# A windowed-attention and feed-forward kernel: two chunks' feed-forward in halves of d_ff, scores two pairs ahead, byte decoding of weights

## The chip, the cores and the metric

The kernel runs on one core of a Trainium2 chip: TensorE (matmuls, into PSUM), VectorE (DVE), ScalarE (ACT), GpSimd (POOL), and SyncE (SP), whose queue issues most of the transfers. The metric is the device time in microseconds of one execution, median of the runs.

## What is computed

Attention with 4 sink positions and a window of 128 over 768 positions, 4 batches, 8 heads of 64 dimensions, then a feed-forward net of d_model 512 and d_ff 2048 on all 3072 tokens. The weights of the net are given as f64.

```python
keep = is_sink | in_window           # pos < 4, or 0 <= i - j < 128
scores = np.where(keep, scale * q @ k.T, -1e9)
a = softmax(scores)
x = (a @ v).transpose(0, 2, 1, 3).reshape(B * S, H * D)
h = x @ w_in
g = np.where(h >= 1, h, np.where(h <= -1, 0.0, (h + 1) ** 2 / 4))
out = g @ w_out
```

## The kernel before

The tokens are cut into 8 chunks of 384 (`CT` = 3 tiles of 128 positions): first half of the sequence for each of the 4 batches, then the second half. A chunk needs 8 *units*, one per head. The result of a chunk's attention lands in `xn` (L245) as four column blocks `ct`, one for each pair of heads.

**Attention of the first 16 units** (chunks 0 and 1) is done in 8 *pairs* of heads, in plain f32: `pair_load` (L408) brings q and k by two transfers, `pair_values` (L418) the values by four, `pair_scores` (L431) multiplies, masks and takes the row's peak on VectorE (L452) and the exponential on ScalarE (L457); `pair_sums` (L460) makes the reciprocals of the row sums; `early_transp` (L468) transposes the probabilities on TensorE, with ScalarE copies out of PSUM (L477, L478, L480); `pair_r` (L498) spreads the reciprocals over 64 partitions by 12 matmuls (L505), `pair_av` (L482) multiplies with the values and VectorE scales the result (L496). The later units take `load`, `scores`, `values`, `transp`, `av`, `sinks` (L254 to L405), in which operands are split into a high and a low part for faster matmuls.

**The feed-forward net** of a chunk is `moe_steps` (L621): four `split`s of `xn` into high and low parts `x` (L618 on ScalarE, L619 on VectorE); then for each of 16 slices `j` of d_ff `stage1` (12 matmuls, L588, 3 for each `ct`; then L595 to L598 and the low part `gl`, L599, which is on POOL for chunk 0 and on VectorE later), and `LAG` = 2 slices behind it `stage2` (9 matmuls, L607, into three PSUM banks `o_ps`, evicted and stored after the last slice, L614, L615). The last two slices' `stage2` are the `tail`, worked in at the start of the next chunk.

**Weights** are f64 in memory. A step `weights(n)` (L194) decodes two slices of `w_in` (n even) or `w_out` (n odd): a transfer of 1 MB (`fetch`, up to two steps ahead, on SP's queue for the first four, on ScalarE's after that), then `decode_parts` (L164): a shift (L170), the sign bits (L176) and the low word's bits (L179) on VectorE, a rounding copy `high` on ScalarE (L180), and the rest on VectorE (L183).

**Order.** TensorE runs in the order in which the program is written. VectorE and ScalarE are ordered by a planner, except where `queue` (L64) chains an instruction behind the one before on its engine. `first_pairs` (L523) writes out pairs 0 to 3, pair 4's scores and four weight steps (`WFIRST`) by hand. After it, `spread` (L637) mixes step lists in proportion to their weights: the feed-forward net of chunk 0 with the other 12 weight steps, and that with pairs 5 to 8 (`pair_steps`, L509) and units 16 and 17. From then on each chunk's feed-forward net is mixed with the attention of the next chunk. `recheck` (L230) loads the weights again and compares their exponents, once per unit from unit 24 (`CHECK`).

## Time and profile before

| | |
|---|---|
| median of 3 runs | 706.29 us (705.91 to 710.62) |
| the profiled execution | 705.98 us |
| its span, first to last instruction | 704.3 us |
| mean granted clock of TensorE | 0.994 |
| TensorE busy | 681.5 us |
| VectorE busy | 510.3 us |
| ScalarE busy | 489.5 us |
| POOL busy | 278.8 us |

The profile is one execution. PE is TensorE's matmuls, PEld its weight loads, which overlap with the matmuls. A group of instructions has its line, its engine, what it writes and reads, and a count; the idle time ahead of it is put down to whatever released it last. The ends of matmuls are modelled, so a matmul that waits behind another also counts as busy. Times within the execution are us from the span's start.

### The profile page before, as it was taken

What the parts mean: (1) busy time and instruction counts of PE and PEld (TensorE: products, weight loads), DVE (VectorE), ACT (ScalarE), POOL (GpSimd) and SP (SyncE); (2) the same over time, 40 slices, a digit from 0 to 9 for tenths busy, and PEclk for the clock granted to TensorE, in tenths of its full rate; (3) what the DMA queues carried; (4) which work ended last, traced back from release to release, by engine and by line L of the source; (5) the groups of instructions that cost most, each with busy time, mean ns of one, the idle gap of its engine ahead of it and who ended that gap; (6) DMA issues with size and microseconds to landing.
All of it is one profiled execution on the core that took longest, in us unless ns stands there. A gap on an engine that the chain in (4) does not pass through costs nothing.

```text
span 704.3 us, 12263 instructions
## 1 busy us (share of the span) xinstructions
PE 681.5 (97%) x3889; PEld 604.6 (86%) x3889; DVE 510.3 (72%) x1405; ACT 489.5 (70%) x1241; POOL 278.8 (40%) x470
## 2 busy tenths in 40 slices
PE   5899998999999999999999999999999999999996
PEld 3567877899999999989889999899899999989995
DVE  7888998887776877688777878878787877642221
ACT  4886667687778868777787877777776876554332
POOL 3003344744443445355554455635544444300000
PEclk9899999999999999999999999999999999999999
DMA  7864533132244344254333443434322310001001
GB/s 232 291 216 156 190 99 135 49 107 60 63 148 124 102 127 129 68 174 128 92 113 105 147 130 124 126 118 133 122 59 62 102 50 22 3 1 45 1 1 49
DMA packets 45441, 73.98 MB, mean 105 GB/s; under 512 B 10744, under 2 KB 30008, under 8 KB 45368
## 3 DMA queue, kind: packets, MB, share of 16 engines
q1 hardware_dynamic: 42104, 60.53, 28.2%
q10 hardware_dynamic: 3264, 12.58, 4.8%
q8 instruction: 33, 0.54, 0.3%
q14 instruction: 40, 0.33, 0.1%
HBM read 66.80 MB, written 6.29 MB: 104 GB/s over the span
## 4 chain that ended last, share of the span: by engine, by line
PE 79%; DVE 9%; DMA 3%; ACT 3%; POOL 3%; issue 2%; SPq 0%; ACTq 0%; POOLq 0%; DVEq 0%
PE h_ps L588 33%; PE o_ps L607 32%; PE ps_a L283 4%; PE ps_a L390 4%; PE ps_a L344 2%; DVE bits L176 2%; DVE bits L179 1%; DMA w<-w_in 1%; POOL q_l L269 1%; PE ps_a L474 1%; DVE w L183 1%; DVE bits L170 1%; PE ps_a L493 1%; DVE p L304 1%; DVE g L597 1%
## 5 line engine op out<-in xcount | busy, mean ns | idle before, releaser
L588 PE MATMUL h_ps<-x,wi 128*128 128x384 f32 x1536 | 310.2, 340 | 0.0
L588 PEld LDWEIGHTS h_ps<-x,wi 128*128 128x128 f32 x1536 | 262.2, 188 | 8.7 <-issue 1.5
L607 PE MATMUL o_ps<-w,gh 128*128 128x512 f32 x768 | 244.0, 398 | 0.0
L607 PE MATMUL o_ps<-w,gl 128*128 128x512 f32 x384 | 151.1, 393 | 0.4 <-POOL gl L599 0.4
L607 PEld LDWEIGHTS o_ps<-w,gh 128*128 128x128 f32 x768 | 134.3, 188 | 16.9 <-issue 1.7
L597 DVE SCALAR_TENSOR_TENSOR g<-g,h_ps 128x384 f32<-128x384 f32 x128 | 70.3, 549 | 61.7 <-ACT g L596 60.6
L595 ACT ACTIVATE g<-h_ps,half 128x384 f32<-128x384 f32 x128 | 73.9, 578 | 52.7 <-PE h_ps L588 52.0
L269 POOL TENSOR_TENSOR q_l<-r,q_h 128x384 fp32r<-128x384 f32 x48 | 51.1, 1064 | 122.7 <-ACT q_h L268 116.1
L598 ACT CAST gh<-g 128x384 fp32r<-128x384 f32 x128 | 65.5, 512 | 46.1 <-DVE g L597 44.9
L290 ACT ACTIVATE p<-p,peak 128x260 f32<-128x260 f32 (+1 forms) x144 | 71.5, 496 | 23.0 <-DVE peak L287 22.4
L607 PEld LDWEIGHTS o_ps<-w,gl 128*128 128x128 f32 x384 | 72.0, 188 | 17.8 <-POOL gl L599 0.7
L599 DVE TENSOR_TENSOR gl<-g,gh 128x384 fp32r<-128x384 f32 x112 | 67.3, 601 | 23.5 <-ACT gh L598 22.6
L267 DVE TENSOR_TENSOR k_s<-k_r,k_s 64x524 fp32r<-64x524 f32 (+1 forms) x44 | 49.1, 1115 | 34.4 <-ACT k_s L265 34.3
L596 ACT ACTIVATE g<-g 128x384 f32<-128x384 f32 x128 | 67.0, 524 | 2.0
L287 DVE CUSTOM_DVE_ANT_0 p<-ps_a,m 128x260 f32<-128x260 f32 (+1 forms) x144 | 57.0, 407 | 14.7 <-PE ps_a L283 13.8
L358 POOL TENSOR_SCALAR_AFFINE_SELECT pt<-pt 128x384 fp32r<-128x384 f32 (+1 forms) x96 | 51.3, 535 | 22.6 <-DVE pt L349 19.5
L304 DVE CUSTOM_DVE_ANT_0 p<-p,stat 128x128 f32<-128x128 f32 x128 | 57.0, 489 | 0.2
L356 POOL TENSOR_SCALAR_AFFINE_SELECT pt<-pt 128x384 fp32r<-128x384 f32 (+1 forms) x96 | 49.9, 521 | 8.8 <-ACT pt L348 4.9
L599 POOL TENSOR_TENSOR gl<-g,gh 128x384 fp32r<-128x384 f32 x16 | 23.4, 1461 | 67.7 <-ACT gh L598 64.2
L390 PEld LDWEIGHTS ps_a<-pt,v_s 128*128 128x128 f32 x304 | 42.4, 190 | 1.8
L390 PE MATMUL ps_a<-pt,v_s 128*128 128x256 f32 (+1 forms) x304 | 41.9, 275 | 0.0
L283 PE MATMUL ps_a<-k_s,q_h 128*128 128x260 f32 (+1 forms) x144 | 40.7, 283 | 1.2 <-DVE sk L352 0.9
(151 smaller groups left out, 933.1 us busy)
## 6 DMA issues: line engine op xcount, KB each, us to landing
r<-qk SPq DMA_DIRECT2D x48, 192.0 KB
k_r<-qk SPq DMA_DIRECT2D x32, 262.0 KB
again<-w_in SPq DMA_DIRECT2D x16, 512.0 KB
again<-w_out SPq DMA_DIRECT2D x16, 512.0 KB
w<-w_in ACTq DMA_DIRECT2D x6, 1024.0 KB
w<-w_out ACTq DMA_DIRECT2D x6, 1024.0 KB
out<-o SPq DMA_DIRECT2D x23, 256.0 KB
r<-vx SPq DMA_DIRECT2D x32, 128.0 KB
```

The source lines that it names most:

```text
L269: nc.gpsimd.tensor_tensor(q_l, q_r, q_h.bitcast(F32), op=ALU.subtract)
L283: nc.tensor.matmul(ps[:, lo:260], lhsT=q[:, i * P:(i + 1) * P], rhs=k_s[:, c0:c0 + 260 - lo], start=(j == 0), stop=(j == len(qs) - 1))
L290: nc.scalar.activation(p[:, i, lo:260], p[:, i, lo:260], AF.Exp, bias=peak_i, scale=-1.0, accum_out=stat[:, i:i + 1])
L304: nc.vector.tensor_tensor_reduce(out=own, in0=own, in1=p[:, i, 0:P], scale=r, scalar=0.0, op0=ALU.add, op1=ALU.add, accum_out=stat[:, i:i ...
L390: nc.tensor.matmul(z, lhsT=w, rhs=y, start=(n == 0), stop=(n == len(mms) - 1))
L588: nc.tensor.matmul(h_ps[:, :T], lhsT=w_i[j][:, w, ct * P:(ct + 1) * P], rhs=x[:, y, ct], start=(ct == 0 and n == 0), stop=(ct == NCT - 1 a ...
L595: nc.scalar.activation(g, h_ps[:, :T], AF.Relu, bias=half, scale=0.5)
L596: nc.scalar.activation(g, g, AF.Square)
L597: nc.vector.scalar_tensor_tensor(g, g, 1.0, h_ps[:, :T], op0=ALU.min, op1=ALU.max)
L598: nc.scalar.copy(gh, g)
L599: (nc.gpsimd if row0 == GL_POOL else nc.vector).tensor_tensor(gl, g, gh.bitcast(F32), op=ALU.subtract)
L607: nc.tensor.matmul(o_ps[tt], lhsT=gg[:, tt * P:(tt + 1) * P], rhs=w_o[j][:, w], start=(j == 0 and n == 0), stop=(j == NJ - 1 and n == 2))
```

## The change

- *Halves of d_ff.* The feed-forward nets of chunks 0 and 1 are done in two halves, slices 0 to 7 and 8 to 15, in the order 0 front, 1 front, 0 back, 1 back. The front's sums go from PSUM to memory (`half_o`, six blocks of 128x512), and are read back and added by VectorE at the end of the back half. Chunk 1 has an `xn1` of its own, so that both can be split again for the back halves.
- *Weights.* Three decodings instead of four in the head, seven in chunk 0's front, four in chunk 1's front, two in chunk 0's back. The transfer of the first steps is no longer ahead of its step.
- *Byte decoding.* The shift and sign steps are replaced by two one-operand byte operations, which write bytes 0 and 3 of each word of `ends`; one two-operand step then makes the word, in place of the low word in the loaded tile.
- *Head.* Scores of pairs 0 and 1 come first, then those of pair m + 2 in step m; decoding and splits are put elsewhere, and the first stage of slices 0 and 1 for blocks `ct` 0 to 2 comes ahead of pair 3's values. The splits of `ct` 0 and 1 copy on POOL; the copies L478 of the first eight heads are on VectorE.
- *Loads.* q and k of a pair or unit in one transfer, a pair's values in one; the sink values need no transfer of their own. Later units' loads are kept behind the pairs' loads. q and v have separate raw tiles.
- *Scaled pairs.* Pairs 5 to 7 scale the probabilities on VectorE ahead of the transposes, need no `pair_r`, and their result is copied by ScalarE.
- `gl` is always on VectorE; the 1e-9 addition of units 16 and 17 is on VectorE; `recheck` begins at unit 26.

```diff
@@ constants
-GL_POOL = 0
-CHECK = range(24, 24 + 2 * NJ)
-WFIRST = 4
+SCALED = range(5, NATIVE // 2)
+CHECK = range(26, 26 + 2 * NJ)
+WFIRST = 3
+WSPLIT = (10, 14)
+HALF = NJ // 2
...
+    def decode_parts(t, ends, words, w, on, early):
...
+        b = words.bitcast(U8).rearrange("p j c (w e) -> p j c w e", e=4)
+        e = ends.rearrange("p j c -> p (j c)").bitcast(U8).rearrange("p (j c e) -> p j c e", j=2, e=4)
...
+            first = nc.vector.tensor_scalar(e[..., 0], b[..., 0, 3], 5, 0x07, op0=ALU.logical_shift_right,
+                                            op1=ALU.bitwise_and)
...
+            second = nc.vector.tensor_scalar(e[..., 3], b[..., 1, 3], 0x80, 0xC0, op0=ALU.bitwise_and,
+                                             op1=ALU.bitwise_xor)
...
+            queue(nc.vector.scalar_tensor_tensor(w, x, 3, ends, op0=ALU.logical_shift_left, op1=ALU.bitwise_xor), early)
...
-            return decode_parts(t, dec.tile([P, 2, DM], I32, name=f"bits{n % 2}"), words, pin=not on, on=on)
+            return decode_parts(t, ends, words, ends if n == NP - 1 else words[..., 0], on, n < WFIRST + 2)
...
-        loaded.append(nc.sync.dma_start(k_s, qkp[b, h // 2, :, T:T + W]).ins)
-        nc.sync.dma_start(q_s, qkp[b, h // 2, :, 0:T])
+        loaded.append(queue(nc.sync.dma_start(qk_s, qkp[b, h // 2, :, :T + W])).ins)
...
+        if m in SCALED:
+            for a in range(2):
+                for i in range(CT):
+                    p = early_p(2 * m + a)[:, i, KB if i == 0 else 0:260]
+                    nc.vector.tensor_scalar(p, p, r[:, a, i:i + 1], None, op0=ALU.mult)
...
+            if u < H:
+                queue(nc.vector.tensor_copy(spn[u % 2][:NSINK], ps[:NSINK, 2 * P:CT * P]))
...
+        for m in (0, 1):
+            for i in range(CT):
+                pair_scores(m, i)
...
+        for m in range(n):
+            pair_load(m + 2)
+            if m < n - 1:
+                wsteps[m + 1][0]()
+            pair_values(m + 1)
+            pair_sums(m)
+            if m == n - 1:
+                head[2][1]()
+                d[m - 1][4]()
+            if 0 < m < WFIRST:
+                block(m)
+            for u in (2 * m, 2 * m + 1):
+                for part in range(2):
+                    early_transp(u, part)
+            if m < n - 1:
+                hold = later if m + 2 == n else None
+                pair_scores(m + 2, 0, hold)
+                pair_scores(m + 2, 1, hold)
+                last = []
+                pair_scores(m + 2, 2, last)
+                pair_r(m)
...
+                if not m:
+                    block(m)
+                else:
+                    d[m - 1][4]()
+                mult = pair_av(m)
+                mult()
+                d[m][3]()
+                if m:
+                    head[m - 1][1]()
+            else:
+                for _, f in head[CT:]:
+                    f()
...
+                pair_r(m)
+                pair_av(m)()
...
-        (nc.gpsimd if row0 == GL_POOL else nc.vector).tensor_tensor(gl, g, gh.bitcast(F32), op=ALU.subtract)
+        nc.vector.tensor_tensor(gl, g, gh.bitcast(F32), op=ALU.subtract)
...
+    def sums_of(row0, tt):
+        o = parts[row0, tt] = moe.tile([P, DM], F32, name="o")
+        nc.sync.dma_start(o, half_o[row0, tt])
...
+            if put == 2:
+                o = parts.pop((row0, tt))
+                nc.vector.tensor_tensor(o, o_ps[tt], o, op=ALU.add)
...
+            if put == 1:
+                half_o[row0, tt] = dram.tile([P, DM], F32, name=f"half{row0}_{tt}")
+                nc.sync.dma_start(half_o[row0, tt], o)
...
+            if put == 2 and tt == 0:
+                sums_of(row0, 2)
...
+        if on and ct < 2:
+            nc.gpsimd.tensor_copy(x[:, 0, ct], xs[:, ct])
...
+    front, back = range(HALF), range(HALF, NJ)
...
+    prev = moe_steps(rows[0], tail, True, xn, front, 1)
+    cut = CT + LAG * (NCT - 1)
+    finish = first_pairs(prev[:cut])
+    pairs = [pair_steps(m) for m in range(5, 9)]
...
+    prev = spread(decoding(WFIRST, WSPLIT[0]), prev[cut + 2 + LAG:], WLEAD)
+    for _, f in spread(pairs, prev, LEAD):
+        f()
+    prev = spread(decoding(*WSPLIT), moe_steps(rows[1], tail, False, xn1, front, 1), WLEAD)
+    for _, f in spread([step for n in (NATIVE, NATIVE + 1) for step in attn_steps(n)], prev, LEAD):
+        f()
+    n0 = NATIVE + 2
+    prev = spread(decoding(WSPLIT[1], NP), moe_steps(rows[0], tail, False, xn, back, 2), WLEAD)
+    prev += moe_steps(rows[1], tail, False, xn1, back, 2)
```

## Rows read from the trace of the kernel before

**Rows 1.** The page, part 1: busy us, share of the span and instructions of each engine.

```profile
PE 681.5 (97%) x3889; PEld 604.6 (86%) x3889; DVE 510.3 (72%) x1405; ACT 489.5 (70%) x1241; POOL 278.8 (40%) x470
```

**Rows 2.** Windows: length; busy (instructions) of PE, PEld, DVE, ACT, POOL; clock, DMA, GB/s.

```profile
0.00:13.00 13.00, 7.62 (x34) 5.37 (x36) 7.80 (x42) 6.13 (x19) 5.59 (x34) 1.00 0.82 255
13.00:44.00 31.00, 23.89 (x199) 16.39 (x196) 28.59 (x79) 24.79 (x81) 0.91 (x2) 0.89 0.78 261
20.00:24.00 4.00, 4.00 (x24) 2.66 (x24) 3.39 (x9) 2.80 (x10) 0.46 (x1) 0.58 0.63 193
44.00:126.00 82.00, 79.84 (x487) 64.24 (x488) 73.02 (x128) 55.05 (x138) 31.70 (x24) 1.00 0.43 148
120.00:130.00 10.00, 8.06 (x42) 6.80 (x41) 8.49 (x25) 6.06 (x17) 7.74 (x10) 1.00 0.43 134
200.00:300.00 100.00, 99.94 (x563) 91.34 (x562) 74.50 (x221) 77.88 (x200) 44.16 (x84) 1.00 0.36 110
```

**Rows 3.** The chain of waits: start us, us, what.

```profile
111.33 1.45 PE ps_a L493 x16
359.68 3.23 DMA r<-vx
689.48 2.08 PE h_ps L588 x12
691.56 6.17 PE o_ps L607 x27
```

**Rows 4.** Groups of VectorE, 0 to 44 us: busy us, mean ns | idle before.

```profile
L176 DVE SCALAR_TENSOR_TENSOR bits<-w,bits 128x1024 int32<-128x1024 int32 x4 | 4.9, 1216 | 0.0
L170 DVE TENSOR_SCALAR bits<-w 128x1024 int32<-128x1024 int32 x4 | 2.6, 662 | 2.9 <-DMA w<-w_in 2.9
L183 DVE TENSOR_TENSOR wi<-bits,wi 128x1024 fp32r<-128x1024 f32 x2 | 2.5, 1226 | 0.8 <-ACT wi L180 0.8
```

**Rows 5.** Timeline of the head: start us, us, engine, line, operation.

```profile
8.50 0.08 DVE L452 DVE_READ_ACCUMULATOR2_ANT peak<- 128x1 f32 x1
14.76 0.28 DVE L452 CUSTOM_DVE_ANT_0 pt<-o_ps,m 128x128 f32<-128x128 f32 x1
15.88 0.08 DVE L452 DVE_READ_ACCUMULATOR2_ANT peak<- 128x1 f32 x1
43.85 1.83 PE L588 MATMUL h_ps<-x,wi 128*128 128x384 f32 x9
```

**Rows 6.** Groups of TensorE, 44 to 130 us; the last one to 140.

```profile
L505 PE MATMUL ps_a<-ident,stat 128*64 128x128 f32 x48 | 3.5, 281 | 0.0
L344 PE MATMUL ps_a<-ident,p 128*128 128x128 f32 x3 | 0.9, 328 | 1.9 <-DVE p L302 1.9
L607 PE MATMUL o_ps<-w,gl 128*128 128x512 f32 x46 | 18.2, 396 | 0.4 <-POOL gl L599 0.4
```

**Rows 7.** Single lines: count, shortest/median/longest ns, first and last start.

```profile
L239 ACT COPY top<-again x32: 637/658/672, 196.7 to 508.7; 128x512 uint8<-128x512 uint8 x32
L614 ACT COPY o<-o_ps x23: 562/587/594, 142.0 to 697.1; 128x512 f32<-128x512 f32 x23
L126 DVE TENSOR_SCALAR m1n<-m1n x1: 285/285/285, 6.3 to 6.3; 128x260 f32<-128x260 f32 x1
L358 POOL TENSOR_SCALAR_AFFINE_SELECT pt<-pt x96: 402/523/1327, 129.8 to 611.4; 128x384 fp32r<-128x384 f32 x64, 128x256 fp32r<-128x256 f32 x32
```

**Rows 8.** Groups of VectorE from 44, of POOL from 0, to 126 us.

```profile
L176 DVE SCALAR_TENSOR_TENSOR bits<-w,bits 128x1024 int32<-128x1024 int32 x12 | 17.0, 1414 | 0.2
L599 POOL TENSOR_TENSOR gl<-g,gh 128x384 fp32r<-128x384 f32 x13 | 19.6, 1506 | 64.5 <-ACT gh L598 61.1 <-PE ps_a L474 3.5
```

**Rows 9.** Timeline of VectorE and POOL at 80 us.

```profile
80.15 1.00 POOL L599 TENSOR_TENSOR gl<-g,gh 128x384 fp32r<-128x384 f32 x1 [4.52 <-ACT gh L598]
80.16 2.07 DVE L176 SCALAR_TENSOR_TENSOR bits<-w,bits 128x1024 int32<-128x1024 int32 x1
81.46 1.67 POOL L267 TENSOR_TENSOR k_s<-k_r,k_s 64x392 fp32r<-64x392 f32 x1 [0.30 <-ACT k_s L265]
```

More of the change, by code (lines that the diff above doesn't have):

```diff
@@ L185, in decode_parts, with word @@
-        return shift, sign, tail, rest_of
-    def decode(t, w, words, pin=False):
-        for f in decode_parts(t, w, words, pin):
-            f()
+            second = nc.vector.tensor_scalar(e[..., 3], b[..., 1, 3], 0x80, 0xC0, op0=ALU.bitwise_and,
+                                             op1=ALU.bitwise_xor)
+            if not on:
+                tc.keep_in_program_order(second)
+            queue(second, early)
+        def word():
+            queue(nc.vector.scalar_tensor_tensor(w, x, 3, ends, op0=ALU.logical_shift_left, op1=ALU.bitwise_xor), early)
@@ L191, in attn_ffn, with high_of @@
+        def high_of():
+            queue(nc.scalar.copy(high, w.bitcast(F32)), early)
+        def rest_of():
+            queue(nc.vector.tensor_tensor(rest, w.bitcast(F32), high.bitcast(F32), op=ALU.subtract), early)
+        return tail, sign, word, high_of, rest_of
     top = {}
@@ L199, in fetch @@
         def fetch():
-            for k in range(n, min(n + min(AHEAD if n > 2 else 1, NP // 2 - n // 2 - 1) + 1, NP)):
+            for k in range(n, min(n + min(AHEAD if n > 2 else 0, max(NP // 2 - 1 - (n + 1) // 2, 0)) + 1, NP)):
                 if k not in raw:
                     raw[k] = wpool.tile([P, 2, 2 * DM], I32, name="w")
-                    with tc.issue_after(loaded[-1]) if k < SYNC else nullcontext():
-                        (nc.sync if k < SYNC else nc.scalar).dma_start(raw[k], src(k))
+                    queue((nc.sync if k < SYNC else nc.scalar).dma_start(raw[k], src(k)), k < SYNC)
         def parts(on):
@@ L623, in moe_steps, with split @@
+    def split(x, xs, ct, on=False):
+        if on and ct < 2:
+            nc.gpsimd.tensor_copy(x[:, 0, ct], xs[:, ct])
+        else:
+            queue(nc.scalar.copy(x[:, 0, ct], xs[:, ct]), on)
+        queue(nc.vector.tensor_tensor(x[:, 1, ct], xs[:, ct], x[:, 0, ct].bitcast(F32), op=ALU.subtract), on)
+    def moe_steps(row0, tail, first=False, xs=xn, js=range(NJ), put=0):
         x = xpool.tile([P, 2, NCT, CT * P], F32R, name="x")
         o_ps, hs = [], {}
-        steps = [(0.0, lambda ct=ct: split(x, ct)) for ct in range(NCT)]
+        steps = [(0.0, lambda ct=ct: split(x, xs, ct, first)) for ct in range(NCT)]
@@ new lines, in moe_steps @@
+        for n, j in enumerate(js):
+            if n < LAG:
+                steps += second[n * CT:(n + 1) * CT]
+            if n >= LAG or not first:
+                steps += [(0.49, lambda j=j, ct=ct: stage1(x, j, ct, hs)) for ct in range(NCT)]
+            if n >= LAG:
+                steps += [(0.65, lambda j=js[n - LAG], tt=tt: stage2(o_ps, hs, j, tt, row0, js, put)) for tt in range(CT)]
+        if put == 2:
+            steps.append((0.0, lambda: (sums_of(row0, 0), sums_of(row0, 1))))
@@ L634, in moe_steps @@
+        tail[:] = [(0.65, lambda j=j, tt=tt: stage2(o_ps, hs, j, tt, row0, js, put)) for j in js[-LAG:]
                    for tt in range(CT)]
@@ new lines, in decoding @@
+    def decoding(a, b):
+        return [(1.0, wsteps[n][2]) for n in range(a, b)]
+    prev = moe_steps(rows[0], tail, True, xn, front, 1)
+    cut = CT + LAG * (NCT - 1)
+    finish = first_pairs(prev[:cut])
+    pairs = [pair_steps(m) for m in range(5, 9)]
+    for m in (2, 3):
+        pairs[m].append((0.0, lambda u=units[NATIVE + m - 2]: load(u)))
+    pairs = [step for steps in pairs for step in steps]
+    hold = []
+    for _, f in prev[cut + 1:cut + 2]:
+        f()
+    pair_load(6)
+    pair_values(5)
```

283 lines of the change are left out of this document (147 added, 136 removed).

## The prediction

> **What bounds the kernel now.** I read the busy totals first. TensorE is busy for 97% of the span, no other engine for more than 72% [rows 1], so at first sight only fewer matmuls would help. But that share is an average, and a busy matmul can be a slow one, so next come the windows [rows 2]. From 200 to 300 us TensorE is busy 99.94 of 100 us with 563 matmuls, and its weight loads take 91 us. From 0 to 44 us it issues 233, and the loads take 22 us (the first two rows together). So there are two regimes: a steady one from about 44 us, in which TensorE is the limit, and a head, in which something else is.
>
> The chain of waits gives the steady pace: 12 first-stage matmuls take 2.08 us, 27 second-stage ones 6.17, the 16 of one pair's values 1.45 [rows 3]. A slice (12 and 9 of them) is then 4.14 us, and the feed-forward net alone 8 chunks x 16 slices x 4.14 = 530 us, which nothing here makes smaller. What can be won lies where TensorE waits.
>
> In the head VectorE is busy 28.59 of the 31 us from 13 to 44 [rows 2], 92%: there it is the limit. Each of its four weight decodings costs 0.66 + 1.22 + 1.22 + 1.23 = 4.3 us (the two two-operand steps alike), and the first had it wait 2.9 us for a weight transfer [rows 4]. Feed-forward work runs from 43.85 us [rows 5]. From 44 to 126 us VectorE is still busy 73 of 82 us, but TensorE 79.8 [rows 2]. Its one long wait up to 130 us is 1.9 us at unit 16's first transposes, for VectorE's scaling L302, with 0.4 us more for a `gl` on POOL behind it [rows 6]; the window 120 to 130 shows that hole, 8.06 of 10 us busy.
>
> **The change, part by part.** All sums are made against the profiled execution, 705.98 us (span 704.3), 0.3 us under the median of 706.29.
>
> *Head, VectorE's queue.* One decoding of four leaves the head: -4.3 us. In the other three a byte operation of 1024 elements takes the place of the shift (0.66) and a second one that of the sign step (1.22). No row shows a byte operation on VectorE. The nearest are the shift itself, one tensor operand read in steps of 8 bytes, at 0.66 us, and the two-operand form at 1.22 [rows 4]. ScalarE's byte copy in the same steps takes 658 ns for 512 elements, against 587 for 512 f32 out of PSUM [rows 7], so bytes as such are not slow. I take 0.66 for each, as they have one tensor operand, and keep 1.22 as the other end: -0.56 per decoding, -1.7 for three. Eight 4x128 copies move from ScalarE to VectorE: between 0.08 (an accumulator read) and 0.28 (128 wide out of PSUM) [rows 5] I take 0.25, +2.0. So 28.6 - 4.3 - 1.7 + 2.0 = 24.6 us of work. Scores of pairs 0 and 1 now both come ahead of any weight, so this work starts where pair 0's reductions end, 8.5 us [rows 5], not at 12.88. At the same 92% it takes 26.7 us, to 35.2. About 2.5 us idle are within that share: pair 0's transposes need ScalarE copies queued behind the exponentials of two pairs.
>
> The last pair does not end with VectorE. From about 34 us TensorE runs 18 first-stage matmuls put ahead of it (18 x 0.173 = 3.1), pair 3's 12 spreading matmuls (0.7), its 16 of values (1.45); then come the multiplication (0.55) and the last split (1.0): 34 + 0.4 + 3.1 + 0.7 + 1.45 + 0.55 + 1.0 = 41.2, with hops 41.5 us. TensorE is then ahead of where it stands at 43.85 today by 15 first-stage matmuls (2.6 us; three run early today too) and some transposes and scores (0.7). Gain: 43.85 - 41.5 + 3.3 = **5.6 us**. Best end 8 (no hops). [...]
>
> *Transfers.* q and k of a pair become one DMA, its values one in place of four. On SP's queue each weight transfer from w1 on stands behind a pair's q and k, which wait for the scores two pairs back. By my order w0 is wanted at 15.4 us and is the fourth transfer, 2.0 MB in all: 8 us at the 255 GB/s of the first 13 us [rows 2]. w1 makes it 3.6 MB, about 15 us, wanted at 19. Cost nothing: VectorE's work on pairs 1 and 2 covers it; without that cover each late weight holds VectorE as the 2.9 us do now.
>
> *Splits on POOL.* Two 128x384 copies; a one-operand 128x384 operation takes POOL 0.52 us [rows 7], and they can run one pair before VectorE needs them: nothing.
>
> *Chunk 0, front half.* Seven decodings stand in it: 7 x (0.66 + 0.66 + 1.22 + 1.23) = 26.4 us. `min/max` and `gl` of 8 slices, all on VectorE now, some 0.46 and 0.5 from start to start: 7.7. Reductions of 2.8 pairs at 1.8 (four within 1.2 us [rows 5], two more): 5.0. Scaling of three pairs, 18 operations whose nearest row is 0.29 for 128x260 [rows 7], 0.22 from start to start: 4.0. Sums and one multiplication: 1.7. Together 44.8 us. TensorE has 78 first-stage (13.5) and 54 second-stage matmuls (12.4) and nearly four pairs at 4.6 to 5: about 44. The engines are even, so I add **+2.0 us** (0 if the two decodings that the front half doesn't use slip into chunk 1, with 4 decodings in 35 us; +5 if TensorE gets only 92%).
>
> *Contention.* A sign step of 1.22 us in the head [rows 4] takes 1.41 on the mean from 44 to 126 us, where POOL runs `gl` at 1506 ns [rows 8], and 2.07 under `gl` and `k_s` [rows 9]. So `gl` adds 16 x 0.5 us to VectorE and gives it back about as much: nothing. [...]
>
> *Spreading matmuls.* Pairs 5 to 7 need none: 48 of four pairs take 3.5 us with overlaps [rows 6], 0.7 per pair, so 2.0 us of TensorE. With VectorE even I count **-1.5** (0 to -2.6).
>
> *The holes at 120 and 134 us.* Unit 16's chain moves into chunk 1's front, where VectorE has room, and its 1e-9 addition from POOL to VectorE. The waits of 1.9 and 0.4 and the slow matmuls around are about 3 us; I count **-2.5** (0 to -3.4).
>
> *Halves.* Six evictions of 0.59 us [rows 7], six stores and six loads of 256 KB more, an addition in place of the last copies. The third sum is asked for when the first result is stored; two transfers like the 3.2 us one on the chain [rows 3] make some 6 us until its bank is free. Its next use is 7 us of matmuls away: hidden, else 1 to 3 us at two places. With two more sets of splits **+0.5** (0 to +4).
>
> *The rest.* Separate raw tiles for q and v take away one wait, behind which a transfer of 3.2 us stands on the chain [rows 3]: **-0.9** (0 to -2). The re-check two units later and the scratch tiles cost nothing.
>
> Sum: -5.6 + 2.0 - 1.5 - 2.5 + 0.5 - 0.9 = -8.0: **698.0 us**.
>
> **The rivals.** *Stepped writes on VectorE.* No row shows a write in steps of 8 bytes, or of bytes. If both byte operations take 1.22 us, a decoding costs 1.1 more; three in the head and the five that the front half needs make 9: 707. With one of them 702 to 703. I put 704. [...] For reads the trace disagrees: L176 reads every second word at 1.22, as L183 does without a step [rows 4].
>
> *Everything is won*: -8 - 2.2 - 3.4 - 0.9 = -14.5, 691.5. For it: TensorE loses little from 44 to 126 us although VectorE is 89% busy [rows 2].
>
> *Slower.* Bytes written into every fourth byte are dearer than any two-operand step. At the longest row's 2.07 us [rows 9] for each of the three steps a decoding takes 7.4, 3.7 over mine; eight of them +29, of which two slices' lead of the second stage behind the first hides some 9: 718. The place is chunk 0's front half, where TensorE waits for banks that VectorE frees late. The gain is gone when the three steps take 3.5 us together instead of 2.5; the kernel is 1% slower from 4.4 on.
>
> **How the numbers follow.** Forecast 0.50 (own range 693 to 703), stepped writes 0.25, everything won 0.15, slower 0.10. Leaving out the best of the third and most of the last gives 689 to 709. About 1%, 7 us, is what a measurement can tell from no change; the line is 699.2. Of the forecast 0.35 lies below it: faster 0.35 + 0.15 = 0.50, same 0.15 + 0.25 = 0.40, slower 0.10.
>
> **What would show it.** Right: feed-forward matmuls from near 34 us, without holes from 41; byte steps of 0.65 to 0.7 us and a word step of 1.22; VectorE over 90% busy from 41 to 87 us with TensorE as full as now; no 2 us hole ahead of unit 16's transposes; no eviction that waits for a partial sum. Wrong: byte steps over 1.2 us, holes ahead of score or transpose matmuls in the front half, or a first stage that starts later than 37 us.

## The result, and the profile after

The changed kernel takes 713.85 us (median of four runs, 712.46 to 715.27) beside 706.10 us of the kernel before on the same chip. The ratio is 1.0107, with a 95% interval of 1.0077 to 1.0137: slower by about one per cent, where 698.0 us was forecast and 709 was the end of the range. The profiled execution took 713.75 us (span 711.7), 7.77 us more than the one of before. One execution of old_decode (below), 841.58 us at a granted clock of 0.75, is left out of its row.

The page of the changed kernel, part 1 (busy us, share of the span, instructions), answers to [rows 1]:

```profile
PE 679.0 (95%) x3853; PEld 602.3 (85%) x3853; DVE 518.7 (73%) x1458; ACT 488.2 (69%) x1239; POOL 250.8 (35%) x455
```

TensorE does 2.5 us less work, in a span that is 7.4 us longer. So the loss is idle time, and the windows say where it lies. Their columns are those of [rows 2]. The changed kernel:

```profile
0.00:44.00 44.00, 32.59 (x254) 23.98 (x255) 33.08 (x125) 28.00 (x89) 7.49 (x36) 0.96 0.67 234
44.00:84.00 40.00, 38.28 (x242) 28.15 (x242) 37.42 (x95) 30.80 (x87) 0.00 (x0) 1.00 0.48 171
84.00:108.00 24.00, 20.91 (x112) 17.60 (x107) 20.14 (x36) 15.13 (x32) 5.24 (x4) 1.00 0.44 145
108.00:130.00 22.00, 21.34 (x110) 18.70 (x109) 19.40 (x37) 14.13 (x32) 8.83 (x11) 1.00 0.30 97
130.00:170.00 40.00, 37.60 (x212) 33.83 (x211) 37.53 (x98) 30.87 (x83) 20.34 (x32) 1.00 0.42 139
222.00:280.00 58.00, 55.75 (x316) 50.07 (x315) 42.79 (x131) 43.01 (x114) 25.78 (x51) 1.00 0.41 137
280.00:620.00 340.00, 337.12 (x1909) 307.65 (x1908) 263.54 (x774) 253.00 (x639) 160.74 (x279) 1.00 0.33 102
620.00:711.70 91.70, 83.36 (x421) 74.85 (x420) 24.73 (x48) 35.70 (x68) 0.00 (x0) 0.97 0.05 19
```

The same stretches of the kernel before:

```profile
0.00:44.00 44.00, 31.51 (x231) 21.76 (x232) 36.40 (x120) 30.92 (x100) 6.50 (x36) 0.92 0.79 260
44.00:84.00 40.00, 40.00 (x244) 31.92 (x244) 34.91 (x60) 26.32 (x67) 12.56 (x9) 1.00 0.47 165
84.00:108.00 24.00, 23.78 (x147) 18.78 (x148) 23.09 (x37) 17.05 (x44) 9.89 (x7) 1.00 0.47 155
108.00:130.00 22.00, 20.06 (x121) 17.16 (x120) 19.02 (x41) 13.20 (x32) 12.61 (x13) 1.00 0.27 91
130.00:170.00 40.00, 39.59 (x222) 35.55 (x222) 32.15 (x92) 31.01 (x83) 22.21 (x37) 1.00 0.25 75
222.00:280.00 58.00, 57.94 (x334) 53.23 (x333) 44.54 (x139) 46.24 (x121) 28.26 (x56) 1.00 0.44 133
280.00:620.00 340.00, 338.90 (x1921) 309.09 (x1920) 260.55 (x765) 252.59 (x635) 164.67 (x273) 1.00 0.32 98
620.00:704.30 84.30, 77.72 (x390) 69.59 (x388) 22.47 (x44) 33.62 (x64) 0.00 (x0) 0.99 0.06 20
```

Take the length less TensorE's busy time, row by row (170 to 222 us is full in both):

| stretch, us | idle before | idle after | more |
|---|---|---|---|
| 44 to 84 | 0.00 | 1.72 | +1.7 |
| 84 to 108 | 0.22 | 3.09 | +2.9 |
| 108 to 130 | 1.94 | 0.66 | -1.3 |
| 130 to 170 | 0.41 | 2.40 | +2.0 |
| 222 to 280 | 0.06 | 2.25 | +2.2 |
| 280 to 620 | 1.10 | 2.88 | +1.8 |
| 620 to the end | 6.58 | 8.34 | +1.8 |

Busy time left for TensorE at 44 us is 681.5 - 31.5 = 650.0 us before and 679.0 - 32.6 = 646.4 after, 3.6 us less: the head and the spreading matmuls together. Then -3.6 + 9.3 (the first six rows) + 1.8 (the end) = +7.4 us, the difference of the spans. There is a gain in the head, smaller than forecast, and it is lost at six places behind it. This says where the time went, not yet why.

What ends TensorE's waits from 44 to 170 us in the changed kernel (waited for: us in total, times, longest us):

```profile
PE o_ps L675 <- DVE gl L663: 2.4, 2, 1.8
PE ps_a L304 <- DVE xn L417: 1.3, 1, 1.3
PE ps_a L304 <- DVE sk L376: 1.1, 1, 1.1
PE ps_a L461 <- DVE peak L472: 1.1, 2, 0.5
PE h_ps L652 <- DVE x L700: 0.9, 1, 0.9
```

These five, the longest, are all VectorE. The timeline of VectorE where the front half of chunk 1 begins (start us, us, engine, line, operation) shows what the first of them stands behind:

```profile
87.51 1.58 DVE L184 TENSOR_SCALAR ends<-w 128x1024 uint8<-128x1024 uint8 x1
88.98 0.76 DVE L191 TENSOR_SCALAR ends<-w 128x1024 uint8<-128x1024 uint8 x1
...
93.17 1.64 DVE L191 TENSOR_SCALAR ends<-w 128x1024 uint8<-128x1024 uint8 x1
94.67 1.36 DVE L700 TENSOR_TENSOR x<-xn,x 128x384 fp32r<-128x384 f32 x1
95.96 0.54 DVE L661 SCALAR_TENSOR_TENSOR g<-g,h_ps 128x384 f32<-128x384 f32 x1
96.43 1.21 DVE L204 TENSOR_TENSOR w<-w 128x1024 fp32r<-128x1024 f32 x1
97.56 1.21 DVE L198 SCALAR_TENSOR_TENSOR w<-w,ends 128x1024 int32<-128x1024 int32 x1
98.70 0.42 DVE L308 CUSTOM_DVE_ANT_0 p<-ps_a,m 128x260 f32<-128x260 f32 x1
...
99.04 0.55 DVE L663 TENSOR_TENSOR gl<-g,gh 128x384 fp32r<-128x384 f32 x1
```

The first new slice's `gl` runs at 99.04 us behind two steps of weight decodings that TensorE does not need yet, and TensorE has nothing else: the old chunk's second stage is used up, and the new one's first matmuls are the ones that need this `gl`.

### The profile page after: what moved, and what is told of

It is laid out like the page before. It is cut to its first block, busy times and chain, and to the rows that moved or that the text cites. A ratio compares the mean times of both kernels' runs of the same rounds, so it can differ in the third digit from the quotient of the medians.

```text
span 711.7 us, 12038 instructions
## 1 busy us (share of the span) xinstructions
PE 679.0 (95%) x3853; PEld 602.3 (85%) x3853; DVE 518.7 (73%) x1458; ACT 488.2 (69%) x1239; POOL 250.8 (35%) x455
## 4 chain that ended last, share of the span: by engine, by line
PE 57%; DVE 22%; ACT 7%; DMA 5%; issue 5%; POOL 2%; ACTq 0%; POOLq 0%; DVEq 0%
PE h_ps L652 24%; PE o_ps L675 23%; PE ps_a L304 3%; PE ps_a L414 3%; DVE gl L663 2%; DVE p L326 2%; DVE w L198 2%; DMA again<-w_in 2%; DVE ends L184 2%; DVE ends L191 2%; DVE g L661 2%; DMA again<-w_out 1%; PE ps_a L368 1%; ACT p L311 1%; DVE w L204 1%
## 5 line engine op out<-in xcount | busy, mean ns | idle before, releaser
L663 DVE TENSOR_TENSOR gl<-g,gh 128x384 fp32r<-128x384 f32 x128 | 81.1, 634 | 27.4 <-ACT gh L662 25.9
L290 POOL TENSOR_TENSOR q_l<-qk_r,qk_s 128x384 fp32r<-128x384 f32 x48 | 52.6, 1096 | 81.5 <-ACT qk_s L289 77.9
L326 DVE CUSTOM_DVE_ANT_0 p<-p,stat 128x128 f32<-128x128 f32 x128 | 61.1, 521 | 0.4
L304 PE MATMUL ps_a<-qk_s 128*128 128x260 f32 (+1 forms) x144 | 40.9, 285 | 6.9 <-DVE sk L376 3.6
L414 PE MATMUL ps_a<-pt,v_s 128*128 128x256 f32 (+1 forms) x304 | 41.5, 273 | 0.0
L288 DVE TENSOR_TENSOR qk_s<-qk_r,qk_s 64x524 fp32r<-64x524 f32 (+1 forms) x44 | 31.5, 716 | 13.0 <-ACT qk_s L286 11.0
L251 POOL COPY again<-peak 1x1 f32<-1x1 f32 x32 | 6.7, 210 | 96.4 <-DVE peak L308 87.5
```

The costliest lines, as they stand in the source:

```text
L304: nc.tensor.matmul(ps[:, lo:260], lhsT=q[:, i * P:(i + 1) * P], rhs=k_s[:, c0:c0 + 260 - lo], start=(j == 0), stop=(j == len(qs) - 1))
L326: nc.vector.tensor_tensor_reduce(out=own, in0=own, in1=p[:, i, 0:P], scale=r, scalar=0.0, op0=ALU.add, op1=ALU.add, accum_out=stat[:, i:i ...
L414: nc.tensor.matmul(z, lhsT=w, rhs=y, start=(n == 0), stop=(n == len(mms) - 1))
L663: nc.vector.tensor_tensor(gl, g, gh.bitcast(F32), op=ALU.subtract)
```

## The experiments

Each ratio below is to the kernel before, run beside it, with its 95% interval. Differences in us are taken between medians; by the ratios they come out up to 1.1 us otherwise. The changed kernel's own is 1.0107 [1.0077, 1.0137], so a single edit worth less than about 3 us can't be told from it by its interval alone; where such an edit is read, it is read from a row. A row is one execution, and not always a typical one: that of sep_loads, sum_buffers and combo_mem is the fastest of its kernel, that of quiet and before_bytes the slowest.

| kernel | us | ratio [interval] |
|---|---|---|
| no_halves | 725.51 | 1.0282 [1.0251, 1.0314] |
| no_halves_free | 722.77 | 1.0243 [1.0224, 1.0261] |
| old_decode | 718.26 | 1.0167 [1.0118, 1.0217] |
| unscaled | 718.22 | 1.0167 [1.0148, 1.0186] |
| gl_pool | 713.01 | 1.0105 [1.0074, 1.0136] |
| no_gl0 | 710.01 | 1.0054 [1.0036, 1.0072] |
| splits_first | 712.41 | 1.0085 [1.0069, 1.0101] |
| quiet | 711.03 | 1.0070 [1.0049, 1.0090] |
| dec_10_16 | 711.37 | 1.0087 [1.0055, 1.0119] |
| klv | 711.01 | 1.0079 [1.0054, 1.0105] |
| sum_buffers | 712.08 | 1.0097 [1.0067, 1.0126] |
| sep_loads | 710.68 | 1.0072 [1.0050, 1.0093] |
| combo_mem | 710.63 | 1.0060 [1.0043, 1.0078] |
| combo | 708.61 | 1.0041 [1.0024, 1.0058] |
| best | 708.45 | 1.0042 [1.0026, 1.0058] |
| best2 | 711.92 | 1.0087 [1.0062, 1.0113] |
| before_bytes | 704.19 | 0.9973 [0.9956, 0.9990] |
| before_bytes_scaled | 719.24 | 1.0179 [1.0161, 1.0197] |

**Parts undone.** First the halves.

```diff
-prev = moe_steps(rows[0], tail, True, xn, front, 1)
+prev = moe_steps(rows[0], tail, True)
...
-prev = spread(decoding(WFIRST, WSPLIT[0]), prev[cut + 2 + LAG:], WLEAD)
+prev = spread(decoding(WFIRST, NP), prev[cut + 2 + LAG:], WLEAD)
```

> Undoes the halves alone: chunk 0 runs all 16 slices with the 13 late decodings, the pairs and units 16 and 17 spread over them, then chunk 1 runs 16 slices; no partial sums, no second splits of the two chunks, all other parts of the change kept (after: 713.85 us). Theory A (VectorE crowding: the dearer byte steps beside POOL and gl on VectorE eat the gain, the halves only shift it): the same VectorE work stands against the same matmuls, so 712 to 715 us, with TensorE's holes back near 120 us. Theory B (the halves cost it: eight more splits of about 1 us, six additions, and VectorE held 2.1 us by a partial sum): 706 to 709 us, and the small holes at 230 to 270 us gone. Theory C (merged loads and the steady part): 711 to 714 us, with the holes at 250 to 270 us still there.

Slower by 11.7 us: none of the three theories. Its trace has one wait of 11 us for unit 17's k, whose load the change fixes in ScalarE's and SP's order. The run was repeated with that order free and with separate raw tiles.

> Undoes the halves as before (725.5 us), but with separate raw tiles for q and k and without the fixed order of unit loads on ScalarE and SP, so that the 11 us wait for unit 17's k does not arise. If that wait was the whole of the 12 us by which the run without halves was slower: 711 to 714 us, the halves neither gain nor cost. If the halves gain by themselves (13 decodings, four pairs and two units do not fit beside 16 slices): 717 to 721 us. If the halves cost: 706 to 710 us.

Still 8.9 us over the changed kernel. What TensorE waits for from 44 to 150 us there:

```profile
PE h_ps L652 <- ACT wi L201: 6.8, 3, 3.7
PE h_ps L652 <- DVE wi L204: 6.4, 4, 2.2
```

These are weights that are not decoded in time. Without halves all 13 late decodings must be done within chunk 0's 16 slices; with halves each decoded weight serves two chunks before the next is due. So the halves do not cost; in this arrangement they gain about 9 us. Theory B, as the main cause, falls.

```diff
-nc.vector.tensor_scalar(e[..., 0], b[..., 0, 3], 5, 0x07, ...)
-nc.vector.tensor_scalar(e[..., 3], b[..., 1, 3], 0x80, 0xC0, ...)
-nc.vector.scalar_tensor_tensor(w, x, 3, ends, op0=ALU.logical_shift_left, op1=ALU.bitwise_xor)
+nc.vector.tensor_scalar(ends, x, 3, 0x3FFFFFFF, op0=ALU.logical_shift_left, op1=ALU.bitwise_and)
+nc.vector.scalar_tensor_tensor(ends, x, -0x40000000, ends, op0=ALU.bitwise_and, op1=ALU.bitwise_or)
+nc.vector.scalar_tensor_tensor(w, low, 29, ends, op0=ALU.logical_shift_right, op1=ALU.bitwise_or)
```

> Decodes as before (shift, sign, low bits: two of the three steps with two operands, 0.66 + 1.22 + 1.22 us) in place of the two byte steps and the word step (0.87 + 0.85 + 1.22 us on the mean up to 120 us); everything else as in the change (713.85 us). If the byte steps save what their undisturbed rows say (about 0.4 us of 3.1 per decoding, seven decodings in stretches where VectorE is full): 716 to 718 us. Theory A in its sharpest form (byte steps are stretched by POOL more than word steps, so they give nothing back): 713 to 715 us.

4.4 us slower by the median of three executions (715.30 to 719.39), just over the range of the first case. The interval overlaps that of the changed kernel, so that the byte decoding gains what its rows say is likely and not shown; nothing speaks for the sharp form of theory A (bytes are stretched more than words).

```diff
-SCALED = range(5, NATIVE // 2)
+SCALED = ()
```

> Pairs 5 to 7 are not scaled on VectorE; TensorE spreads their reciprocals as for the other pairs (36 matmuls, some 2.1 us), and VectorE multiplies three times in place of 18 scalings (about 4 us less, 1.7 us more); everything else as in the change (713.85 us). If VectorE's full stretch from 60 to 100 us sets the pace: 711.5 to 713 us. If TensorE does there: 715 to 716 us.

4.4 us slower, more than either case. Its windows show why the price is larger than TensorE's 2 us: from 84 to 108 us TensorE is idle 5.2 us, with one wait of 3.8 us for the first new slice's `gh`. Without scaling pair 7 ends with spreading matmuls, a copy and a multiplication, so the splits of chunk 1 start later (93.07 instead of 90.91 us) and the boundary's chain is that much longer.

**gl.** Chunk 0's 16 `gl`, once back on POOL and once left out.

```diff
-nc.vector.tensor_tensor(gl, g, gh.bitcast(F32), op=ALU.subtract)
+(nc.vector if row0 else nc.gpsimd).tensor_tensor(gl, g, gh.bitcast(F32), op=ALU.subtract)
```

> Puts gl of chunk 0's sixteen slices back on POOL, as in the kernel before; everything else as in the change (713.85 us). Theory A: VectorE is full from 60 to 100 and from 130 to 160 us and sheds 16 x 0.69 us, but POOL's 1.5 us operations stretch VectorE's: if the shed work counts, 709 to 712 us. If it is given back by stretched steps, as my prediction took it: 713 to 715 us. Theory B (halves) has no part in it: 713 to 715 us.

```diff
+gl = gh
+if row0:
+    gl = moe3.tile([P, T], F32R, name="gl")
+    nc.vector.tensor_tensor(gl, g, gh.bitcast(F32), op=ALU.subtract)
```

> Leaves out gl of chunk 0's sixteen slices (its matmuls read gh a second time, so chunk 0's output lacks that correction); everything else as in the change (713.85 us). VectorE sheds 16 x 0.55 to 0.7 us between 44 and 165 us with nothing put on POOL. If VectorE's sum sets the pace there: the TensorE holes at 95 to 100 and 140 to 160 us shrink by 4 to 6 us in all, 708 to 710 us, clearly under the run with gl on POOL (713.0 us). If only the order at the boundaries counts: 711 to 713 us, no better than gl on POOL.

On POOL nothing is gained (713.0), left out 3.8 us (710.0). The window 44 to 170 us, first the kernel before, then the changed one, `gl` on POOL, `gl` left out, and the kernel before with byte decoding (below):

```profile
44.00:170.00 126.00, 123.43 (x728) 103.41 (x729) 109.17 (x227) 87.58 (x224) 57.27 (x63) 1.00 0.37 122
```

```profile
44.00:170.00 126.00, 118.13 (x667) 98.28 (x666) 114.49 (x263) 90.93 (x232) 34.41 (x47) 1.00 0.42 143
```

```profile
44.00:170.00 126.00, 117.16 (x660) 97.77 (x660) 109.53 (x247) 89.93 (x227) 51.77 (x61) 1.00 0.42 143
```

```profile
44.00:170.00 126.00, 119.82 (x677) 99.78 (x676) 106.95 (x254) 92.42 (x235) 32.23 (x48) 1.00 0.41 143
```

```profile
44.00:170.00 126.00, 124.41 (x728) 104.96 (x729) 102.06 (x226) 87.99 (x225) 53.47 (x63) 0.99 0.36 118
```

VectorE works 114.5 of 126 us in the changed kernel, 109.2 before. But without `gl` it works less than before (107.0), and TensorE is still idle 126 - 119.8 = 6.2 us, where it was 2.6 before. So VectorE's sum is a part (7.9 to 6.2 us of idle time in this window), not the whole: at a lower load the new arrangement still loses 3.6 us more than the old one. And of the 4.2 us between the two traced executions only these 1.7 lie where the edit acts; from 222 to 620 us, where no `gl` was left out, TensorE is idle 3.4 us in place of 5.1.

**Order at the boundaries.**

```diff
-prev = spread(decoding(*WSPLIT), moe_steps(rows[1], tail, False, xn1, front, 1), WLEAD)
+prev = moe_steps(rows[1], tail, False, xn1, front, 1)
+prev = prev[:NCT] + spread(decoding(*WSPLIT), prev[NCT:], WLEAD)
```

> Puts the four splits of a chunk ahead of the decodings that are spread over its slices, at chunk 1's front half and at chunk 0's back half; everything else as in the change (713.85 us; there the first decoding of each stretch is written ahead of the splits, and at 88 to 95 us VectorE runs four byte steps and a word step, 6 us, before the fourth split at 94.67 us). Theory A as a matter of order: the fourth split comes some 3 us earlier and the TensorE hole at 95 to 100 us shrinks by 2 to 3 us: 711 to 712 us. Theory A as a matter of sum (VectorE full whatever the order): the hole moves behind the splits, 713 to 714.5 us.

The fourth split came 3 us earlier (91.63 us), the hole stayed: TensorE then waited 2.2 us for `gl`, behind the same decodings, and 712.41 us lies in neither range. Here the stretch lost more than its idle time: TensorE was busy 1.4 us from 94 to 98, the mean granted clock from 84 to 108 us was 0.86, and a single second-stage matmul behind the hole took 0.63 to 0.80 us, against 0.39 to 0.40 ahead of it. So there were 96 matmuls in the 24 us from 84, where the changed kernel, at 1.00, has 112. In klv (below) it is the same, 0.86 with 94. In combo (below) the clock stayed at 1.00 (110 matmuls) with a wait of 2.5 us at the same place, so no run shows that the hole is what lowers the clock. The next run moves the decodings themselves (`prev[:quiet]` with 25 steps ahead of them in place of 4).

> The four decodings of chunk 1's front half start after its first three slices instead of ahead of them; everything else as in the change (713.85 us). If the hole at 95 to 100 us is a matter of order (the first slice's gl stands behind two decodings' steps on VectorE): no wait of TensorE for gl there, 84 to 108 us TensorE busy 23 of 24 us instead of 20.9, 710.5 to 712 us. If VectorE's sum decides: the hole moves to 105 to 125 us, 713 to 715 us.

The windows of quiet, and then of best, which has the same start:

```profile
84.00:108.00 24.00, 23.09 (x126) 20.23 (x127) 18.90 (x38) 16.30 (x38) 5.72 (x4) 1.00 0.44 157
108.00:170.00 62.00, 58.05 (x307) 51.31 (x306) 59.57 (x134) 45.78 (x110) 31.75 (x43) 0.97 0.36 124
```

```profile
84.00:108.00 24.00, 23.83 (x124) 21.24 (x123) 18.91 (x40) 15.86 (x37) 2.52 (x2) 1.00 0.37 128
108.00:170.00 62.00, 57.49 (x312) 50.52 (x312) 59.23 (x139) 45.32 (x111) 30.06 (x42) 1.00 0.40 128
```

The hole at 95 us is a matter of order: TensorE's 84 to 108 us goes from 20.9 to 23.1 us busy, as expected, with one wait of 0.8 us for `gl` left. But from 108 to 170 us its idle time then grows from 3.06 (0.66 + 2.40, above) to 3.95 us, in best to 4.51, with VectorE over 59 of 62 us busy. Of 2.2 us won (2.9 in best) 0.9 (1.5) are given back behind it: the first theory is right for the place, the second for a part of the sum of both places.

Two more edits of the same stretch, `WSPLIT = (10, 16)` and `KL_POOL = range(0)`:

> Puts the last two decodings into chunk 1's front half (six there, none in chunk 0's back half); everything else as in the change (713.85 us). Theory A, that VectorE is overloaded where decodings meet attention units at full rate (9.8 of 10 us busy from 130 to 160 us, TensorE 8.86 and 8.74 of 10 in two of these windows): the holes at 140 and 160 us go, and as VectorE is 87% busy from 110 to 130 us only part returns: 711 to 712.5 us. Rival, that the front half of chunk 1 has no room either: the hole at 95 to 100 us grows by as much, 713.5 to 716 us.

> Takes the k subtraction of units 16 to 19 from POOL to VectorE; everything else as in the change (713.85 us). If POOL's operations are what stretches VectorE's steps at 87 to 96 us (byte steps 1.58 and 1.64 us against 0.75, the split 1.36 against 0.55): these steps fall back towards 0.75 and 0.55, the added four operations cost VectorE about 0.7 us each, the hole at 95 us shrinks, 712.5 to 713.5 us. If VectorE's sum alone decides: four operations more in a full stretch, 714.5 to 716.5 us.

Both came out faster than the changed kernel by 2.5 and 2.8 us, within what the intervals leave undecided. In klv the first byte step and the fourth split fell to 0.77 and 0.56 us, as expected (the second byte step, still beside a POOL operation, took 1.60), but the hole at 95 us stayed (2.9 us), so the stretch of those two did not make it, and the gain is not the one expected. In dec_10_16 one decoding instead of two is left from 130 to 170 us, and TensorE is idle 1.66 us there instead of 2.40; 1.9 us more are the end of the run (below).

**Transfers.** A place of its own for the third partial sum, and its load two slices earlier:

```diff
-o = parts[row0, tt] = moe.tile([P, DM], F32, name="o")
+o = parts[row0, tt] = third[0]() if tt == 2 else moe.tile([P, DM], F32, name="o")
...
-if put == 2 and tt == 0:
+if put == 2 and j == js[-LAG] and tt == 0:
     sums_of(row0, 2)
```

> The third partial sum gets a tile of its own and its load is issued two slices earlier, so that it no longer waits for the first result's store; everything else as in the change (713.85 us). Theory B (the wait for partial sums holds VectorE's in-order queue, 2.1 us at 230 us): the addition's idle time before it falls from 2.1 us to under 0.3, the 230 to 240 us window fills to 10 us, 711.5 to 713 us. Theories A and C: no change beyond 0.7 us.

In the changed kernel the addition stood thus in VectorE's timeline:

```profile
229.92 0.69 DVE L680 TENSOR_TENSOR o<-o_ps,o 128x512 f32<-128x512 f32 x1 [2.08 <-DMA o<-half]
```

In sum_buffers no wait for a partial sum is left from 222 to 236 us, for VectorE or TensorE. The time is 1.8 us lower, inside the expected range, and not told apart by the interval.

```diff
-qk_r = att1.tile([P, QK], F32, name="qk_r")[:, :T + W]
+q_r = att1.tile([P, T], F32, name="q_r")
+k_r = att1.tile([P, P + CT * KB], F32, name="k_r")[:, :W]
...
-pin(nc.sync.dma_start(qk_r, qk[b, h, t0 // CT, :, :T + W]), u)
+pin(nc.sync.dma_start(k_r, qk[b, h, t0 // CT, :, T:T + W]), u)
+pin(nc.sync.dma_start(q_r, qk[b, h, t0 // CT, :, :T]), u)
```

> Loads a unit's q and k with two transfers into two raw tiles, as the kernel before did, in place of one transfer into one tile; everything else as in the change (713.85 us). Theory C (the merged tile is held until q's last reader on POOL, so the next unit's load and its casts come later, and score matmuls wait): TensorE's busy time from 280 to 620 us rises from 337.1 to over 339 us, the holes at 255 and 263 us go, 710.5 to 712 us. Theories A and B: 713 to 715 us.

The windows of sep_loads:

```profile
222.00:280.00 58.00, 56.47 (x322) 51.26 (x321) 43.48 (x138) 43.78 (x116) 26.82 (x54) 1.00 0.44 139
280.00:620.00 340.00, 338.95 (x1926) 310.45 (x1925) 262.51 (x769) 254.35 (x639) 159.65 (x276) 1.00 0.32 100
```

From 280 to 620 us TensorE is idle 1.05 us in this trace, as before (1.10), against 2.88, as theory C had it; the end of the run (below) is 3.6 us in place of 5.4. But this trace is the fastest of nine executions (707.18 us, median 710.68), and other traces do not bear the price out. The same stretch of klv, with the merged tile, and of best, with separate tiles:

```profile
280.00:620.00 340.00, 338.65 (x1926) 310.24 (x1925) 262.94 (x776) 254.04 (x641) 162.09 (x280) 1.00 0.33 102
```

```profile
280.00:620.00 340.00, 337.36 (x1914) 308.19 (x1913) 261.72 (x766) 252.77 (x637) 159.09 (x275) 1.00 0.32 100
```

klv is idle 1.35 us, best 2.64. Over all traces it is 1.35 to 3.34 us in the eleven with the merged tile (mean 2.39), 1.05 to 2.64 in the six with separate tiles (1.98), 1.10 to 1.85 in the three of the kernel before and its variants (1.58). That the merged tile costs 1.8 us is not shown; on the mean it is 0.4, less than the spread. A hole of 1.2 us at about 262 us stays, so that half of the expectation failed.

**Parts alone, in the kernel before.**

> The kernel before (706.1 us) with the byte decoding alone: two byte steps and a word step in place of shift, sign and low bits, one word tile and one tile of ends for its two bit tiles; gl of chunk 0 stays on POOL. If a decoding saves 0.4 us as the undisturbed rows say (0.66 + 1.22 + 1.22 against 0.74 + 0.74 + 1.22): four in the head and a freer VectorE up to 126 us, 703 to 704.5 us. If TensorE sets the pace after the head anyway and the head waits for transfers: 704.5 to 706.5 us. If POOL's 1.5 us operations stretch byte steps more than word steps: 706 to 708 us.

704.19 us: faster by 0.27%, and the fastest kernel here; the interval excludes no change, though it is less than one per cent.

> The kernel before (706.1 us) with byte decoding (704.2 us as measured alone) and with pairs 5 to 7 scaled on VectorE, without the spreading matmuls of these pairs. If the scaling gains in the kernel before as in the change (there 4.4 us): 700 to 702 us. If VectorE, 88% busy from 44 to 126 us there, gives it back: 703.5 to 706 us.

15 us slower than the same kernel without scaling. What TensorE waits for from 44 to 130 us there:

```profile
PE ps_a L496 <- DVE pt L486: 7.8, 3, 4.9
PE ps_a L496 <- DVE p L486: 2.6, 1, 2.6
```

L486 is the scaling, L496 the transposes behind it. TensorE's fixed order stands still because the scalings come late on VectorE; beside the halves the same part gains 4.4 us. That the 12 decodings in chunk 0, against seven with the halves, are what makes the scalings late is argued and not run. The worth of this part hangs on the others.

**Together.** combo_mem is sep_loads, sum_buffers and splits_first; combo adds `WSPLIT = (10, 16)` and klv; best has quiet in place of splits_first and `WSPLIT = (10, 15)`; best2 adds decoding 3 in the 4.2 us that VectorE waits ahead of pair 3's values, with `WSPLIT = (11, 16)`.

> The change with three of the single edits together: separate raw tiles for q and k, a tile of its own for the third partial sum, splits ahead of the decodings. If they recover different holes: 713.85 - 3.2 - 1.8 - 2 = 707 us; if they overlap: 709 to 711 us.

> As the three edits together, and also the last two decodings in chunk 1's front half and the k subtractions of units 16 to 19 on VectorE. If all five recover different holes: 713.85 - 3.2 - 1.8 - 2 - 2.5 - 2.8 = 701.5 us. If the stretch from 84 to 130 us is limited by VectorE's sum, the last two add nothing to the other three: 707 to 711 us.

> The change with the quiet start of chunk 1, separate raw tiles for q and k, a tile of its own for the third partial sum, the k subtractions of units 16 to 19 on VectorE, and five decodings in chunk 1's front half. The five edits with splits first in place of the quiet start took 708.6 us. If the quiet start recovers its hole (2 to 3 us): 705.5 to 707 us. If VectorE's sum decides from 84 to 130 us: 708 to 710 us.

> The version of 708.45 us, and decoding 3 in the 4.2 us that VectorE waits at the end of the head (37 to 41 us), so that the stretch from 44 to 165 us holds one decoding less, with five in chunk 1's front half and none in chunk 0's back half. If VectorE's sum sets the pace: 705 to 706.5 us. If the holes come from order and from TensorE's banks: 708 to 709 us.

combo and best are 5 us faster than the change, and their intervals lie below its own; they stay 0.4% above the kernel before. The edits overlap: -12 was their plain sum. best2 is a miss. It took a decoding out of the full stretch and came out 3.5 us slower than best; in its trace TensorE waits 2.9 us for `xn` (VectorE) near 140 and 152 us, where the last decoding, meant for chunk 1's front half, had slipped to 147 us.

## Why the prediction was wrong, point by point

*Head, -5.6, and spreading matmuls, -1.5: the gains came, about half of them counts in the sum.* The timeline of the changed kernel:

```profile
35.50 3.37 PE L652 MATMUL h_ps<-x,wi 128*128 128x384 f32 x18
...
42.57 0.42 PE L652 MATMUL h_ps<-x,wi 128*128 128x384 f32 x1
```

The 18 matmuls start at 35.5 instead of 34.4 us, the rest at 42.57 instead of 41.5, so by the prediction's formula 43.85 - 42.57 + 3.3 = 4.6 us. By counts that fits: up to 44 us 24 first-stage matmuls are issued, against 4, and 12 spreading matmuls are left, against 48, which at the steady pace is 20 x 0.173 + 36 x 3.5 / 48 = 6.1 us. But TensorE's busy time left at 44 us fell by 3.6 us only, where the two terms had 7.1. Some matmuls behind 44 us are busy longer, such as 24 score matmuls of the last pairs (4.3 us before, 5.3 after); why is open. From 40 to 50 us ScalarE is the fuller engine (8.3 of 10 us busy, VectorE 6.0), but TensorE's own wait there, 1.1 us, is for VectorE's `peak`; which of them holds the order back is not shown. Within the change the scaling, without which the spreading matmuls return, is worth 4.4 us, since it shortens the chain to chunk 1's first split.

*Byte and word steps: the kind held, the size not quite.* Groups of VectorE in the changed kernel from 44 to 170 us:

```profile
L198 DVE SCALAR_TENSOR_TENSOR w<-w,ends 128x1024 int32<-128x1024 int32 x12 | 14.6, 1217 | 0.0
L663 DVE TENSOR_TENSOR gl<-g,gh 128x384 fp32r<-128x384 f32 x22 | 13.8, 632 | 0.7 <-ACT gh L662 0.6
...
L184 DVE TENSOR_SCALAR ends<-w 128x1024 uint8<-128x1024 uint8 x13 | 11.1, 857 | 0.1
L191 DVE TENSOR_SCALAR ends<-w 128x1024 uint8<-128x1024 uint8 x13 | 11.0, 847 | 0.0
```

The rival of the stepped writes, put at 704, is out: no run shows stepped writes that are dearer. The two byte steps take 857 and 847 ns on the mean here, not 1.22 us, and the word step writes every second word at 1217 ns, as the step of before did without one (1216, [rows 4]). The slower rival, dear byte writes, did not happen either: the three steps take 2.9 us, not 4.4. But the sum had 2.5: a byte step takes 0.75 us where nothing disturbs it, not 0.66, and 0.85 on the mean of this stretch. For 13 decodings that is 5 us of VectorE more than was counted, in the stretch where VectorE proved full.

*Chunk 0's front half, +2.0: held.* TensorE is idle 1.7 us more from 44 to 84 us.

*Contention, 0: held.* `gl` on VectorE costs it about 10 us more (22 x 0.632 against six before), and the other two-operand steps fall back from 1414 ns [rows 8] to 1217. gl_pool, 0.8 us lower and not told apart, does not speak against it.

*The holes at 120 and 134 us, -2.5: the step that failed first.* These holes went (108 to 130 us: 1.94 to 0.66 us idle). But the step said that the work moves into "chunk 1's front, where VectorE has room". It has none where that half begins: 17 instructions fill all of the 10 us from 90 to 100, steps of two decodings among them, and a new hole of 2.9 us stands at 95 us. From 84 to 130 us the forecast of -2.5 became +1.6. quiet and best show that the decodings ahead of the first slices make this hole: with them moved, 0.9 and 0.2 us are left of the 3.1 from 84 to 108 us. The sum had the front half of chunk 0 in full and never made one for the first slices of the next.

*What had no term: decodings beside attention at full rate.* Seven decodings were counted into chunk 0's front half; the last two, in chunk 0's back half, were not priced. There (130 to 170 us) VectorE goes from 32.2 to 37.5 of 40 us busy, and TensorE's idle time from 0.4 to 2.4 us. They are a part of it and chunk 0's `gl` on VectorE another: one decoding less leaves 1.7 us (dec_10_16), no `gl` 1.1 (no_gl0).

*Halves, +0.5: about right, as far as these runs show.* The third sum was held to be hidden, since TensorE's next use of the bank is 7 us away. It was not quite: TensorE waited 0.6 us for it, while VectorE stood 2.1 us ahead of the addition (2.08, above) and started nothing else in that time. From 222 to 236 us TensorE is idle 0.7 us, and in sum_buffers nothing. But its idle time from 222 to 280 us grows by 2.2 us. TensorE's longest waits there, in the changed kernel and then in no_halves, which has no partial sums:

```profile
PE ps_a L304 <- DVE sk L376: 1.2, 1, 1.2
PE o_ps L675 <- DVE o L680: 0.6, 1, 0.6
```

```profile
PE ps_a L304 <- DVE sk L376: 1.2, 1, 1.2
```

The longer wait, 1.2 to 1.4 us, is in this stretch of the changed kernel and of all 16 variants of it, without halves, without scaling and with separate tiles alike, and in none of the three traces of the kernel before and its variants. So it comes from a part of the change that no run took back; which one stays open.

*The rest, -0.9: not seen.* The prediction looked at the tile that q and v had shared and at the wait behind it [rows 3], and not at the new sharing of q and k: one tile, free only when POOL has made `q_l`. TensorE's idle time from 280 to 620 us grows by 1.8 us between the two traces, by 0.8 on the means given above; the merged tile is not shown to be the cause.

*The end: in no step.* SP's own wait behind the last stores, at the branch around the general code, in the changed kernel and then in the kernel before:

```profile
SPq L879 <- SPq L879: 5.4, 2, 3.7
```

```profile
SPq L751 <- SPq L751: 3.6, 1, 3.6
```

Two waits instead of one, 1.8 us. Some variants have two (sum_buffers, klv, quiet, no_gl0: 5.0 to 6.1 us), some one (dec_10_16, sep_loads, combo_mem, combo, best, best2: 3.4 to 3.9), without an edit near that line. The changed kernel has two waits and 39 packets on the instruction queue q14, the kernel before one wait and 40 packets. Why there are two stays open.

Put together, the forecast beside the rows of the two traces (work left at 44 us, then idle time):

| term of the sum | stretch, us | forecast | measured |
|---|---|---|---|
| head, spreading matmuls | to 44 | -7.1 | -3.6 |
| chunk 0's front half | 44 to 84 | +2.0 | +1.7 |
| the holes | 84 to 130 | -2.5 | +1.6 |
| none (chunk 0's back half) | 130 to 170 | 0 | +2.0 |
| halves | 222 to 280 | +0.5 | +2.2 |
| the rest | 280 to 620 | -0.9 | +1.8 |
| none (the end) | from 620 | 0 | +1.8 |
| sum | | -8.0 | +7.5 |

The difference, 15.5 us, is nearly all of the 15.8 between forecast and outcome (698.0 to 713.75, the profiled execution). So the places are known; the largest miss is the holes, 4.1 us, and the cause of the new hole in it is shown. Of the other rows the decodings and `gl` are a part of 130 to 170 us and the third sum is 0.7 us of 222 to 280; the causes of the head's short gain, of the 1.2 us wait, of 280 to 620 us and of the end stay open. Open also is how the loss from 44 to 170 us divides between VectorE's sum and its order: each edit that filled one hole opened part of another, and none of the combinations took that stretch back to the 2.6 us of before.

## What to carry to other kernels

When work is moved out of a full stretch, make the same sum for the stretch that takes it, slice by slice at its start: where a new block begins, only its first slices' chain feeds the bottleneck engine, and any long operation queued ahead of them on the engine that makes their operands stands in that chain (here the steps of two decodings on VectorE, and a hole of 2.9 us). A wait that the bottleneck engine can sit out may still stop the engine that meets it, and all that is queued there (VectorE 2.1 us here, TensorE 0.6). Price the parts of a combined change together: here scaling gains 4.4 us within the change and costs 15 in the kernel before with byte decoding. And before a row of one trace is called the price of an edit, read the same row in the other traces: from 280 to 620 us they differ by 2 us among kernels with the same code for it.
